# Float32 iotas, a causal select and the wide pattern's distances on GpSimd, and later size tests, in a local-attention and channel-mix kernel

## The chip, the core and the metric

The kernel runs on one core of a Trainium2 chip. The metric is the device time of one execution in microseconds. The engines are TensorE (PE, with its weight loads as PEld), VectorE (DVE), ScalarE (ACT), GpSimd (POOL) and SyncE (SP), which issues most DMAs.

## What is computed

Attention over 4 x 8 heads of 768 positions and 64 channels, with a local window, a few global positions and a distance bias, and behind it a channel mix of width 512 and 1024. `n_global` is 8 and `n_local` is 96, both given as 64-bit integers at run time.

```python
scores = q @ k.T / sqrt(D)
rel = pos[:, None] - pos[None, :]
is_global = pos[None, :] < n_global
is_local = (rel >= 0) & (rel < n_local)
dist = where(is_global & ~is_local, n_local, abs(rel))
scores = where(is_global | is_local, scores - slopes[h] * dist, -1e9)
x = softmax(scores) @ v                     # heads side by side: B, S, 512
xk, xr = (mu * x + (1 - mu) * x_prev for mu in (mu_k, mu_r))
out = sigmoid(xr @ w_r) * (relu(xk @ w_k) ** 2 @ w_v)
```

## The kernel before

A tile is 128 queries; there are 24 of them, 6 for each batch. A tile sees at most 232 keys: 8 global ones, the 96 before it, and its own 128. Per tile and pair of heads (`hp`), TensorE makes scores (L421 and L422 in the first six tiles, L424 and L425 later), VectorE adds the bias pattern and takes the row's extreme (L430), ScalarE exponentiates with the sum (L431), TensorE transposes (L461, named t_0 to t_3 by head pair), ScalarE copies the result out (L465), and TensorE multiplies by v (L486). Two tiles make a chunk of 256 columns for the channel mix: `mix` makes xk and xr (L520) and splits each into a high part (L521, ScalarE) and a low part (L522, VectorE); `channel_mix` multiplies them by the weights in three passes (L531 to L533: kp, z, vps).

The weights arrive as 64-bit words. Ten blocks (4 of w_k, 2 of w_r, 4 of w_v) are turned into floats by VectorE in three operations (L210, L211, L212 on `wa`), and split into high (L216, ScalarE) and low parts (L234 on VectorE, or L230 to L232 through TensorE). This happens in tiles 0 to 5, beside the attention of those tiles.

The bias patterns come first of all. `btmp` holds pieces of scratch: from iotas (GpSimd) come the distances; `dist0` (L149) makes `pat0`, the pattern of a batch's first tile (128 keys, L153 and L155), and `dist` (L163 to L166) makes `pat`, the wide pattern of all other tiles (232 keys, L170 on ScalarE and L172 on GpSimd, four heads each). FAR is 1e12. `read_sizes` (L78 to L80) turns the two sizes into floats. L806 to L811 test whether the sizes fit this path; the result is used at the end (L812), to choose a general path, `wide`, which does not run here. `PLAN["GO"]` names the tile and head pair behind whose L430 these tests are put; here (1, 1).

What each engine does in which order is set by a scheduler that places the instructions of all engines by a timeline of its own; `issue_after` bounds it, and SP's queue is kept in program order in the first six steps. SP's loads there are: q and k of tile 0, of tile 1, v of tile 0, two blocks of w_k, q and k of tile 2, v of tile 1, two more blocks of w_k, and so on. The q and k tiles of the first six tiles have only every second partition loaded, and the others are cleared once, by a fill on some engine (`zero_fill`, L306 to L311) that the load waits for. `ident` and `minus` (L83, L85) are identity matrices. The first ten matmuls of the kernel (L116) work on zeros and give nothing.

Of the kernel before, what the change touches and what calls it, by code (L numbers as in the profile page):

```python
# [12 lines left out]
I32 = mybir.dt.int32  # L13
U32 = mybir.dt.uint32
AF = mybir.ActivationFunctionType
ALU = mybir.AluOpType
# [9 lines left out]
GMAX = 8  # L26
BACK = 96
LMAX = BACK + 1
W = GMAX + BACK + 128
OWN = GMAX + BACK  # L30
# [13 lines left out]
    "Z": {('q', 0): 'D', ('q', 1): 'A', ('k', 1): 'A'},  # L44
    "P0": 'DADDADAD',
    "GD": 0,
    "GO": (1, 1),
    "PT": 'PAPAPAPA',
    "BEHIND": {},
    "WB": {},  # L50
# [7 lines left out]
FAR = 1.0e12  # L58
# [4 lines left out]
def tile_biased_attention_channel_mix(ctx: ExitStack, tc: tile.TileContext, qT, kT, v, n_sizes, mu_kr, w_k, w_v, w_r, q_rows, k_rows, v_rows, slopes, out):  # L63
    nc = tc.nc
    vec, act, pool, pe = nc.vector, nc.scalar, nc.gpsimd, nc.tensor
# [8 lines left out]
    ngf, nlf = sizes[:, 0:1], sizes[:, 1:2]  # L74

    def read_sizes():
        low, high = words[:, :, 0], words[:, :, 1]
        vec.tensor_copy(words, sizes_w)  # L78
        vec.scalar_tensor_tensor(sizes, low, 0.0, high, op0=ALU.is_lt, op1=ALU.add)
        vec.scalar_tensor_tensor(sizes, sizes, 4294967296.0, low, op0=ALU.mult, op1=ALU.add)  # L80
# [47 lines left out]
    def piece():  # L128
        edge.append(next(cut))
        return btmp[:, edge[-2] : edge[-1]]  # L130

    ints, flts, local, glo, dist0, dist = (piece() for _ in range(6))
    ints = ints.bitcast(I32)
    j = flts[:, 224:352]

    pool.iota(ints[:, 96:224], [[-1, 128]], base=0, channel_multiplier=1)
    pool.iota(ints[:, 224:352], [[1, 128]], base=0, channel_multiplier=0)
    pool.iota(ints[:, 0:96], [[-1, 96]], base=96, channel_multiplier=1)
    vec.tensor_copy(flts, ints)
    causal = flts[:, 96:224]  # L140
    vec.tensor_scalar(dist0, causal, 0.0, FAR, op0=ALU.is_lt, op1=ALU.mult)
    vec.tensor_max(causal, causal, dist0)
    read_sizes()


# [14 lines left out]
    with ExitStack() as later:  # L160
        if PLAN.get("GD"):
            later.enter_context(tc.issue_after(first_done.ins))
        vec.tensor_scalar(local[:, 0:96], flts[:, 0:96], nlf, FAR, op0=ALU.is_ge, op1=ALU.mult)  # L163
        vec.tensor_copy(dist[:, OWN:W], local[:, 96:224])
        vec.tensor_scalar(dist[:, 0:GMAX], glo[:, 0:GMAX], nlf, None, op0=ALU.max)
        vec.tensor_add(dist[:, GMAX:OWN], local[:, 0:96], flts[:, 0:96])  # L166
    for h in range(H):
        c = -8.0 * 2.0 ** -(h + 1)
        if PLAN.get("PT", "PAPAPAPA")[h] == "A":
# [695 lines left out]
```

## Time and profile before

| | |
|---|---|
| median of 3 runs | 495.69 us (495.29 to 499.2) |
| the profiled execution: its own time | 496.69 us |
| the profiled execution: its span | 494.9 us |
| PE busy | 485.4 us (98%), 3614 instructions |
| PEld busy | 432.0 us (87%) |
| DVE busy | 349.7 us (71%), 839 instructions |
| ACT busy | 335.7 us (68%), 852 instructions |
| POOL busy | 205.5 us (42%), 331 instructions |
| HBM read, written | 53.55 MB, 6.29 MB |

The span runs from the first to the last instruction of the core. Busy times are averages over a start, in which patterns and weights are made, and a long steady part. Matmuls are pipelined and their ends are modelled, so a busy PE is not PE at its peak.

### The profile page before, as it was taken

What the parts mean: (1) busy time and instruction counts of PE and PEld (TensorE: products, weight loads), DVE (VectorE), ACT (ScalarE), POOL (GpSimd) and SP (SyncE); (2) the same over time, 40 slices, a digit from 0 to 9 for tenths busy, and PEclk for the clock granted to TensorE, in tenths of its full rate; (3) what the DMA queues carried; (4) which work ended last, traced back from release to release, by engine and by line L of the source; (5) the groups of instructions that cost most, each with busy time, mean ns of one, the idle gap of its engine ahead of it and who ended that gap; (6) DMA issues with size and microseconds to landing.
All of it is one profiled execution on the core that took longest, in us unless ns stands there. A gap on an engine that the chain in (4) does not pass through costs nothing.

```text
span 494.9 us, 10286 instructions
## 1 busy us (share of the span) xinstructions
PE 485.4 (98%) x3614; PEld 432.0 (87%) x3614; DVE 349.7 (71%) x839; ACT 335.7 (68%) x852; POOL 205.5 (42%) x331
## 2 busy tenths in 40 slices
PE   8799999999999999999999999999999999999997
PEld 5579898898988998998998998998998998898986
DVE  7989997867677677677687686677768764464541
ACT  8889967648488568477487477576587577686370
POOL 4201051646465554644655635635546525203000
PEclk9999999999999999999999999999999999999999
DMA  6988162620616306406405405504503216656311
GB/s 237 376 284 346 35 129 82 165 88 2 172 24 160 90 7 171 115 1 162 129 1 145 129 1 136 156 1 121 152 21 103 85 23 185 213 199 227 128 43 50
DMA packets 22587, 60.59 MB, mean 122 GB/s; under 512 B 3296, under 2 KB 4576, under 8 KB 22016
## 3 DMA queue, kind: packets, MB, share of 16 engines
q1 hardware_dynamic: 22384, 59.85, 40.8%
q8 instruction: 31, 0.51, 0.4%
q14 instruction: 28, 0.23, 0.2%
q10 hardware_dynamic: 144, 0.00, 0.0%
HBM read 53.55 MB, written 6.29 MB: 121 GB/s over the span
## 4 chain that ended last, share of the span: by engine, by line
PE 92%; DVE 3%; DMA 2%; ACT 1%; issue 1%; ACTq 0%
PE vps L531 9%; PE vps L533 9%; PE vps L532 9%; PE kp L531 9%; PE kp L532 9%; PE kp L533 9%; PE av L486 8%; PE t L461 8%; PE z L531 4%; PE z L532 4%; PE z L533 4%; PE s L425 3%; PE s L424 3%; DMA qz<-in_qT_dram 2%; PE s L422 2%; PE s L421 1%
## 5 line engine op out<-in xcount | busy, mean ns | idle before, releaser
L449 POOL TENSOR_SCALAR e<-e,r 128x232 f32<-128x232 f32 (+1 forms) x144 | 68.8, 497 | 121.1 <-DVE r L443 83.1
L431 ACT ACTIVATE e<-e,nmax 128x232 f32<-128x232 f32 (+1 forms) x192 | 89.6, 469 | 37.4 <-DVE nmax L430 36.9
L531 PE MATMUL kp<-xk_hi,wk 128*128 128x256 f32 x384 | 107.9, 282 | 0.0
L532 PE MATMUL kp<-xk_lo,wk 128*128 128x256 f32 x384 | 107.3, 280 | 0.0
L533 PE MATMUL kp<-xk_hi,wk 128*128 128x256 f32 x384 | 107.2, 280 | 0.0
L430 DVE CUSTOM_DVE_ANT_0 e<-s,pat 128x232 f32<-128x232 f32 (+1 forms) x192 | 64.2, 374 | 30.4 <-PE s L425 27.1
L531 PE MATMUL vps<-wv,kk_hi 128*128 128x512 f32 (+1 forms) x200 | 76.8, 385 | 0.0
L533 PE MATMUL vps<-wv,kk_lo 128*128 128x512 f32 (+1 forms) x200 | 76.7, 383 | 0.0
L532 PE MATMUL vps<-wv,kk_hi 128*128 128x512 f32 (+1 forms) x200 | 76.4, 382 | 0.0
L532 PEld LDWEIGHTS kp<-xk_lo,wk 128*128 128x128 f32 x384 | 72.1, 188 | 0.8 <-DVE xk_lo L522 0.2
L531 PEld LDWEIGHTS kp<-xk_hi,wk 128*128 128x128 f32 x384 | 72.0, 188 | 0.7 <-ACT xk_hi L521 0.3
L533 PEld LDWEIGHTS kp<-xk_hi,wk 128*128 128x128 f32 x384 | 72.1, 188 | 0.0
L465 ACT COPY et<-t 128x256 f32<-128x256 f32 (+1 forms) x176 | 53.3, 355 | 25.1 <-PE t L461 24.9
L461 PE MATMUL t<-ident,e 128*128 128x128 f32 x352 | 54.5, 275 | 1.5 <-ACT et L465 1.4
L562 DVE TENSOR_TENSOR kk<-kp,kk 128x512 f32<-128x512 f32 x48 | 32.9, 687 | 29.7 <-ACT kk L561 29.4
L564 DVE TENSOR_TENSOR kk_lo<-kk,kk_hi 128x512 fp32r<-128x512 f32 x48 | 35.7, 747 | 24.0 <-ACT kk_hi L563 23.2
L461 PEld LDWEIGHTS t<-ident,e 128*128 128x128 f32 x352 | 40.3, 135 | 7.3 <-ACT et L465 1.6
L563 ACT CAST kk_hi<-kk 128x512 fp32r<-128x512 f32 x48 | 29.8, 623 | 21.9 <-DVE kk L562 21.6
L533 PEld LDWEIGHTS vps<-wv,kk_lo 128*128 128x128 f32 x200 | 37.6, 188 | 7.5
L531 PEld LDWEIGHTS vps<-wv,kk_hi 128*128 128x128 f32 x200 | 37.6, 189 | 6.7 <-ACT pat L576 0.2
L532 PEld LDWEIGHTS vps<-wv,kk_hi 128*128 128x128 f32 x200 | 37.7, 189 | 6.5
L424 PE MATMUL s<-kw,qh 128*128 128x232 f32 (+1 forms) x144 | 40.4, 306 | 0.0
(121 smaller groups left out, 1071.4 us busy)
## 6 DMA issues: line engine op xcount, KB each, us to landing
qraw<-in_qT_dram SPq DMA_DIRECT2D x36, 256.0 KB
kraw<-in_kT_dram SPq DMA_DIRECT2D x36, 256.0 KB
out_dram<-sig SPq DMA_DIRECT2D x23, 256.0 KB
va<-in_v_dram SPq DMA_DIRECT2D x20, 240.0 KB
vb<-in_v_dram SPq DMA_DIRECT2D x20, 208.0 KB
w<-in_w_k_dram SPq DMA_DIRECT2D x4, 1024.0 KB
w<-in_w_v_dram SPq DMA_DIRECT2D x4, 1024.0 KB
again<-in_w_k_dram SPq DMA_DIRECT2D x8, 512.0 KB
```

Source lines behind the costliest of these rows:

```text
L424: pe.matmul(o, s["qh"][:, h, :], s["kw"][:, h, c0:W], start=True, stop=False)
L430: biased[n, hp] = vec.tensor_tensor_reduce(out=e[:, :w], in0=o, in1=p[:, h, :], op0=ALU.add, op1=ALU.min, scale=-0.125, scalar=3.0e38, acc ...
L431: act.activation(e[:, :w], e[:, :w], AF.Exp, bias=s["nmax"][:, h : h + 1], scale=-1.0, accum_out=s["sum"][:, h : h + 1])
L449: pool.tensor_scalar(e[:, :w], e[:, :w], r[:, u : u + 1], 1.0, op0=ALU.mult, op1=ALU.mult)
L461: s["turned"] = pe.transpose(pt[0:p, c : c + 128], e[:, k * 128 : k * 128 + p], ident)
L465: act.copy(dst, pt[0:p, k * 256 : k * 256 + 256].rearrange("p (u q) -> p u q", u=2)[:, :, q:128])
L486: pe.matmul(o, vt[:, h * 64 : (h + 1) * 64], et[0:p, c : c + 128 - q], start=k == 0, stop=k == nb - 1)
L531: pe.matmul(o, sh, mh, start=first, stop=False)
L532: pe.matmul(o, sh, ml, start=False, stop=False)
L533: return pe.matmul(o, sl, mh, start=False, stop=last)
L562: vec.tensor_mul(kk, pv, kk)
L564: rest = vec.tensor_sub(kkl[:, 2 * fp : 2 * fp + 2, :], kk, kkh[:, 2 * fp : 2 * fp + 2, :])
```

## The change

The iotas write float32 at once, so that the cast L139 falls away. The causal part, "FAR where the key lies ahead of the query", is a select on GpSimd in place of two VectorE operations. The four operations that make `dist` go to GpSimd, two of them in a form with a second factor of 1.0. The size tests are put behind L430 of tile 8 in place of tile 1.

```diff
-    "GO": (1, 1),
+    "GO": (8, 1),
...
-    pool.iota(ints[:, 96:224], [[-1, 128]], base=0, channel_multiplier=1)
-    pool.iota(ints[:, 224:352], [[1, 128]], base=0, channel_multiplier=0)
-    pool.iota(ints[:, 0:96], [[-1, 96]], base=96, channel_multiplier=1)
-    vec.tensor_copy(flts, ints)
+    def count(o, step, base, channel):
+        pool.iota(o, [[step, o.shape[1]]], base=base, channel_multiplier=channel, allow_small_or_imprecise_dtypes=True)
+
     causal = flts[:, 96:224]
-    vec.tensor_scalar(dist0, causal, 0.0, FAR, op0=ALU.is_lt, op1=ALU.mult)
-    vec.tensor_max(causal, causal, dist0)
+    count(causal, -1, 0, 1)
+    pool.affine_select(causal, causal, [[-1, 128]], ALU.is_ge, FAR, base=0, channel_multiplier=1)
+    count(j, 1, 0, 0)
+    count(flts[:, 0:96], -1, 96, 1)
     read_sizes()
...
-        vec.tensor_scalar(local[:, 0:96], flts[:, 0:96], nlf, FAR, op0=ALU.is_ge, op1=ALU.mult)
-        vec.tensor_copy(dist[:, OWN:W], local[:, 96:224])
-        vec.tensor_scalar(dist[:, 0:GMAX], glo[:, 0:GMAX], nlf, None, op0=ALU.max)
-        vec.tensor_add(dist[:, GMAX:OWN], local[:, 0:96], flts[:, 0:96])
+        pool.tensor_scalar(local[:, 0:96], flts[:, 0:96], nlf, FAR, op0=ALU.is_ge, op1=ALU.mult)
+        pool.tensor_add(dist[:, GMAX:OWN], local[:, 0:96], flts[:, 0:96])
+        pool.tensor_scalar(dist[:, 0:GMAX], glo[:, 0:GMAX], nlf, 1.0, op0=ALU.max, op1=ALU.mult)
+        pool.tensor_scalar(dist[:, OWN:W], local[:, 96:224], 1.0, 1.0, op0=ALU.mult, op1=ALU.mult)
```

The scheduler then orders other work differently too, in about the first 115 us. Three places show it, each as a difference of one engine's order, with - for before and + for the change.

ScalarE at its very start, where it clears the q and k tiles of tile 1 (qz_182 and kz_183, each in two halves) and makes `minus`:

```order
 L309 ACT_TABLE_LOAD
 L309 CAST qz_182<-zeros 128x512 x2
-L309 CAST kz_183<-zeros 128x512 x2
+L309 CAST kz_183<-zeros 128x512
 L85 ACTIVATE minus<-ident 128x128
+L309 CAST kz_183<-zeros 128x512
 L153 ACTIVATE pat_137<-btmp 128x128 x3
 L170 ACTIVATE pat<-btmp 128x232 x4
```

The second half of the k fill now stands behind L85.

TensorE at the change from tile 1 to tile 2: t_0_370 and t_1_389 are transposes of tile 1, s_0_378 and s_1_397 are scores of tile 2, whose L421 needs the q load of tile 2 (qz_178):

```order
 L461 MATMUL t_0_370<-ident,e_1_287 128x128
 L461 MATMUL t_0_370<-ident,e_1_287 104x128
+L421 MATMUL s_0_378<-kz_183,qz_178 128x104
+L421 MATMUL s_1_397<-kz_183,qz_178 128x104
 L461 MATMUL t_1_389<-ident,e_2_316 128x128
 L461 MATMUL t_1_389<-ident,e_2_316 104x128
 L461 MATMUL t_1_389<-ident,e_3_319 128x128
 L461 MATMUL t_1_389<-ident,e_3_319 104x128
-L421 MATMUL s_0_378<-kz_183,qz_178 128x104
-L421 MATMUL s_1_397<-kz_183,qz_178 128x104
```

The two L421 have moved ahead of the four transposes t_1 of tile 1.

VectorE in tile 4, behind the L430 of its third head pair (e_5): wa_621, wa_724 and wa_848 are the weight blocks 6, 7 and 8, e_6 and e_7 the last two heads of tile 4, and xk_lo is the low part of the first chunk:

```order
+L210 TENSOR_SCALAR wa_848<-w_8_788 128x1024
+L212 SCALAR_TENSOR_TENSOR wa_621<-w_6_600,wa_621 128x1024
 L430 ISA e_6_868,nmax_599<-s_3_863,pat 128x232
 L430 ISA nmax_599 128x1
 L430 ISA e_7_871,nmax_599<-s_3_863,pat 128x232
 L430 ISA nmax_599 128x1
-L212 SCALAR_TENSOR_TENSOR wa_621<-w_6_600,wa_621 128x1024
-L522 TENSOR_TENSOR xk_lo<-mix_k,xk_hi 128x1024
-L210 TENSOR_SCALAR wa_848<-w_8_788 128x1024
 L212 SCALAR_TENSOR_TENSOR wa_724<-w_7_664,wa_724 128x1024
+L522 TENSOR_TENSOR xk_lo<-mix_k,xk_hi 128x1024
+L211 SCALAR_TENSOR_TENSOR wa_848<-w_8_788,wa_848 128x1024
```

L210 on block 8 and L212 on block 7 stood behind xk_lo and now stand ahead of it, and L212 on block 6 stands ahead of e_6 and e_7.

## Rows read from the trace of the kernel before

**Rows 1.** Busy time by stretch: stretch, its length, busy per engine (instructions), granted clock, DMA share, GB/s.

```profile
core 0: us, PE busy (x) PEld busy (x) DVE busy (x) ACT busy (x) POOL busy (x), PEclk, DMA share, GB/s
6.00:7.00 1.00, 1.00 (x8) 0.87 (x8) 1.00 (x6) 0.98 (x5) 0.71 (x2) 1.00 0.55 111
...
13.00:17.60 4.60, 1.80 (x15) 1.30 (x13) 4.20 (x15) 3.54 (x16) 1.79 (x2) 1.00 1.06 333
17.60:50.80 33.20, 33.08 (x285) 26.48 (x285) 31.74 (x76) 29.48 (x85) 4.57 (x5) 1.00 0.88 321
...
54.70:450.00 395.30, 395.30 (x2982) 357.81 (x2982) 281.01 (x655) 271.37 (x670) 189.15 (x296) 1.00 0.38 104
```

**Rows 2.** Waits of PE after 40 us: total us, times, longest.

```profile
PE s L421 <- issue: 1.0, 1, 1.0
PE row L269 <- DVE worst L267: 0.3, 1, 0.3
```

**Rows 3.** Chain that ended last, in order of time: start us, us, what.

```profile
8.84 8.69 DMA qz<-in_qT_dram
...
480.75 0.23 PE vps L532
```

**Rows 4.** Timeline 0 to 8 us: start, us, engine, line, operation [idle before <- releaser].

```profile
1.06 4.45 PE L116 MATMUL idle<-zeros 128*128 128x512 bf16 x10 [1.06 <-DVE zeros L113]
...
1.52 0.29 POOL masks.py:199 TENSOR_SCALAR_AFFINE_SELECT ident<-ident 128x128 f32<-128x128 f32 x1
1.79 1.84 POOL L306 MEMSET kz<- 128x1024 f32 x2
2.00 1.87 DVE L139 CAST btmp<-btmp 128x352 f32<-128x352 int32 x1
3.52 1.13 ACT L309 CAST kz<-zeros 128x512 f32<-128x512 bf16 x2
4.56 0.31 ACT L85 ACTIVATE minus<-ident 128x128 fp32r<-128x128 f32 x1
4.68 0.47 SPq L339 DMA_DIRECT2D kz<-in_kT_dram  x1
...
6.21 1.71 POOL L172 TENSOR_SCALAR pat<-btmp 128x232 bf16<-128x232 f32 x4 [2.30 <-DVE btmp L164]
6.63 1.24 ACT L170 ACTIVATE pat<-btmp 128x232 bf16<-128x232 f32 x4
7.09 0.28 DVE L430 CUSTOM_DVE_ANT_0 e<-s,pat 128x128 f32<-128x128 f32 x1
7.99 0.25 POOL L297 TENSOR_SCALAR k_first<-kz 128x64 f32<-128x64 f32 x1
```

**Rows 5.** Timeline 14 to 28 us, PE, POOL and DVE.

```profile
14.94 1.21 POOL L297 TENSOR_SCALAR kz<-k_first 128x64 f32<-128x64 f32 x1
15.54 0.66 PE L461 MATMUL t<-ident,e 128*128 128x128 f32 x4 [1.39 <-ACT et L465]
17.66 0.66 PE L421 MATMUL s<-kz,qz 128*128 128x104 f32 x4 [1.47 <-DMA qz<-in_qT_dram]
20.32 0.14 DVE L811 TENSOR_SCALAR okf<-okf 128x1 f32<-128x1 f32 x1
20.39 0.38 DVE L430 CUSTOM_DVE_ANT_0 e<-s,pat 128x232 f32<-128x232 f32 x1
27.43 0.40 DVE L430 CUSTOM_DVE_ANT_0 e<-s,pat 128x232 f32<-128x232 f32 x1 [1.11 <-PE s L422]
```

**Rows 6.** Timeline 53 to 57 us, DVE and PE.

```profile
53.44 1.21 DVE L522 TENSOR_TENSOR xk_lo<-mix_k,xk_hi 128x1024 fp32r<-128x1024 f32 x1
54.57 0.68 DVE L210 TENSOR_SCALAR wa<-w 128x1024 int32<-128x1024 int32 x1
54.70 0.38 PE L532 MATMUL kp<-xk_lo,wk 128*128 128x256 f32 x1
55.17 1.21 DVE L212 SCALAR_TENSOR_TENSOR wa<-w,wa 128x1024 int32<-128x1024 int32 x1
56.31 0.39 DVE L430 CUSTOM_DVE_ANT_0 e<-s,pat 128x232 f32<-128x232 f32 x1
```

More of the change, by code (lines that the diff above doesn't have):

```diff
@@ L130, in piece @@
         return btmp[:, edge[-2] : edge[-1]]
-    ints, flts, local, glo, dist0, dist = (piece() for _ in range(6))
-    ints = ints.bitcast(I32)
+    _, flts, local, glo, dist0, dist = (piece() for _ in range(6))
     j = flts[:, 224:352]
-    pool.iota(ints[:, 96:224], [[-1, 128]], base=0, channel_multiplier=1)
-    pool.iota(ints[:, 224:352], [[1, 128]], base=0, channel_multiplier=0)
-    pool.iota(ints[:, 0:96], [[-1, 96]], base=96, channel_multiplier=1)
-    vec.tensor_copy(flts, ints)
+    def count(o, step, base, channel):
+        pool.iota(o, [[step, o.shape[1]]], base=base, channel_multiplier=channel, allow_small_or_imprecise_dtypes=True)
     causal = flts[:, 96:224]
-    vec.tensor_scalar(dist0, causal, 0.0, FAR, op0=ALU.is_lt, op1=ALU.mult)
-    vec.tensor_max(causal, causal, dist0)
+    count(causal, -1, 0, 1)
+    pool.affine_select(causal, causal, [[-1, 128]], ALU.is_ge, FAR, base=0, channel_multiplier=1)
+    count(j, 1, 0, 0)
+    count(flts[:, 0:96], -1, 96, 1)
     read_sizes()
```

## The prediction, made before the change was run

> **What bounds the kernel now.** I read the stretches first, then what TensorE waited for, then the chain, then the start row by row. In the table by stretch, TensorE is busy 395.30 of the 395.30 us from 54.70 on, 33.08 of 33.20 between 17.60 and 50.80, but only 1.80 of 4.60 before 17.60 [rows 1]. After 40 us it waits twice, 1.0 us and 0.3 us [rows 2]. So nearly everything behind 54.7 us is matmuls end to end: what is lost or won before that time is carried to the end, and nothing behind it can give much back. The change works in the first 60 us, where three things set the pace.
>
> First, the vector work on the patterns: the cast L139 takes 1.87 us and the first biased scores (L430) begin at 7.09, behind the pattern work [rows 4]. Second, the loads: the chain spends 8.69 us on the q load of tile 2, issued at 8.84 [rows 3]; it lands behind the first two blocks of w_k, and TensorE stands 1.47 us before L421 starts at 17.66, having stood 1.39 us just before [rows 5]. Third, VectorE's weight work: from 27.43 on it has no row with an idle time ahead of it worth naming; at 53.44 it makes xk_lo, done at 54.65, and TensorE's first matmul on xk_lo starts at 54.70 [rows 6]. From there TensorE never waits again. So the question is: when does VectorE finish xk_lo, and when does the q load of tile 2 land?
>
> **The change part by part.**
>
> *The start.* L139 goes (1.87 us [rows 4]), with L141, L142 and the four operations of the wide pattern, so VectorE reaches L430 earlier. It cannot before the first scores exist, which wait for a k load at about 5.9; from 7.09 that is 0.8 us or a little more. What is late next is the q load of tile 2. Its issue waits for TensorE's scores of tile 0, so it moves up by the same 0.8 us, but the queue's order ahead of it is unchanged and the engines are full: DMA share 1.06 up to 17.60 [rows 1]. I therefore let it land where it does, and the 0.8 us become a longer wait of TensorE: worth nothing (bounds: 0 and -0.8).
>
> *GpSimd's share.* The iotas keep their count. The causal select is not in the trace; ident's select on the same 128x128 shape takes 0.29 [rows 4]. The four operations of the wide pattern run on GpSimd instead: 0.39 to 0.43 each by L172 (1.71 for four of 128x232) [rows 4], about 1.6 us and done near 6 us; ScalarE takes up its half of that pattern (L170) at 6.63 now [rows 4], so no loss. The upper bound is the 128x64 copy at 14.94 that took 1.21 us beside VectorE's work, against 0.25 for the one at 7.99 [rows 4, 5]: four of those are 4.8 us. I take the low end, since L172 has the same form and ran while VectorE made its own patterns; the other is a rival.
>
> The Trainium skill (SBUF — State Buffer, Who interferes with whom) says VectorE and GpSimd share a port pair as an exclusive lock, so whoever comes second waits for the other's whole instruction. The trace agrees: L139 overlaps GpSimd's two fills and ends 0.24 us after them. By the rule the four moved operations and VectorE's short ones take turns, which would eat the 0.8 us at the start and leave the sum as it is.
>
> *The k fill.* ScalarE clears the k tile in two halves (1.13 us for both), and L85 follows; SP issues that tile's k load at 4.68, when the fill is done [rows 4]. The new order puts L85 (0.31) between the halves. The loads have a gap just there (DMA share 0.55 from 6 to 7 us [rows 1]) and everything behind queues up, w_k and the q load of tile 2 included: +0.25 us (bounds 0 and 0.31).
>
> *The size tests.* L806 to L811 leave VectorE's early work. Two of them stand before a wait and are free; four cost what they push back the next row, as L811 at 20.32 does to L430 at 20.39 [rows 5]: 0.07 each, -0.25 us in all (at most 4 x 0.14). In tile 8 they cost the same on a VectorE that is not waited for.
>
> *What the scheduler does with it.* TensorE's transposes t_1 of tile 1 now stand behind the L421 that waits for the q load, so 0.44 us of work that ran before the wait runs after it; the scores of tile 2's second half come earlier, so VectorE's 1.11 us wait at 27.43 [rows 5] shrinks. But TensorE is busy 33.08 of 33.20 [rows 1] and has work added, so of the 1.11 I credit only -0.2 (bounds 0 and -1.1). The term that matters: two weight operations that followed xk_lo now precede it. L210 on block 8 takes 54.57 to 55.17, L212 on block 7 55.17 to 56.31 [rows 6]: +1.74 us on VectorE ahead of xk_lo, while TensorE has only tile-5 scores and transposes to do, and the second of these also wait for L430s that stand behind L210 and L212. The bound below is nothing, if TensorE still had 1.74 us of work at that point; but now it starts 0.05 us after xk_lo is done, so I take it all.
>
> The sum: 0 + 0.25 - 0.25 - 0.2 + 1.74 = +1.5 us on xk_lo, kept to the end. The profiled execution took 496.69 us (span 494.9), 1.0 above the median of 495.69; that run would take 498.2, and the median goes to **497.2 us**. By its own bounds the sum runs from +0.2 to +2.0: 495.9 to 497.7.
>
> **The rivals.**
>
> *The early start survives.* If the q load lands 0.8 us earlier with its issue, and the 1.74 us find cover, the kernel gains: 495.69 - 0.8 = 494.9 us, or about no change where only one of them holds. For it: TensorE did wait 1.47 us on just that load. Against: the saturated queue, and the 0.05 us at 54.7.
>
> *TensorE's clock falls.* Now TensorE stands from 14.15 to 15.54, runs t_1 for 0.66 us, and stands again until L421 at 17.66 [rows 5]. Moved behind L421, t_1 leaves TensorE with nothing from about 13.8 to 17.9: 4 us instead of two waits of 1.4 and 1.5. At the kernel's start ten matmuls of 512 columns took 4.45 us [rows 4], the pace of 1.2 GHz; one of 512 columns at 480.75 takes 0.23, that of 2.4 GHz [rows 3]. If the clock fell in the longer gap and took as long as then to rise, TensorE would lose half of 4.45: 497.2 + 2.2 = 499.4 us. It decides only if the gap really closes up to 4 us; both present waits left the granted clock at 1.00 [rows 1]. The Trainium skill (TensorE: Matmul & The Clock Gate, HAM oscillation — how this bites in real kernels) has the clock fall back when matmuls wait for a DMA too long; no row here shows a fall.
>
> *The wide pattern comes late.* With four operations of 1.21 us, it is done at 4.2 + 4.8 = 9.0, and ScalarE's L170 (1.24), which stands ahead of all its exponentials, ends at 10.3 instead of 7.87. ScalarE has 1.06 us idle before 17.60 [rows 1], so some 1.3 us remain: 498.5 us. It decides above 0.6 us per operation.
>
> *More than 5 us lost* would take several such stops; I see no place for it.
>
> **How the numbers follow.** The forecast 0.57; the early start, whole or in part, 0.23; the clock 0.12; the late pattern 0.04; the rest 0.04. The range to hold 8 in 10: from 494.7, a little under the first rival, to 499.5, over the second. One per cent of this kernel, 5 us, is about what a measurement tells from no change. Only the upper end of the clock rival and a part of the rest reach it: faster 0.02, same 0.92, slower 0.06.
>
> **What would show it.** Right: L430's first start near 6.3; L421 of tile 2 still at 17.5 to 18.0 with a wait of some 4 us ahead of it; xk_lo finished near 56, TensorE idle just before, and full from there on. Wrong: L421 of tile 2 before 17.2 (the loads were not what held it); xk_lo's first matmul at or before 54.7; a granted clock under 1.00 after 17 us; L170 ending after 8 us; or a TensorE wait of over 0.5 us behind 60 us, where I counted none.

## The result, and the profile after

The changed kernel takes 500.21 us (median of 22 runs, 496.07 to 502.06); the kernel before, timed beside it, 496.24 us (22 runs, 494.64 to 499.9). The ratio is 1.0056, 95% interval 1.0036 to 1.0077. It is smaller than the ratio of the two medians (1.0080), as the times of each kernel fall into two groups, on which more below, and the changed kernel has most of its runs in the slower one; the ratio of the means is 1.0061. That is slower by some 2.8 us, clear of the noise but within the one per cent that counts as no change. On the 495.69 us from which the forecast was made, the ratio gives 498.5 us: 1.3 above the forecast of 497.2 and inside the range of 494.7 to 499.5. The median of 500.21 itself lies above that range, since the kernel before is 0.55 us slower here and the medians lie further apart than the ratio says. The profiled execution took 500.58 us with a span of 498.7 us (before: 496.69 and 494.9), so 3.8 us have to be found.

By stretch (columns as in [rows 1]):

```profile
core 0: us, PE busy (x) PEld busy (x) DVE busy (x) ACT busy (x) POOL busy (x), PEclk, DMA share, GB/s
13.00:17.60 4.60, 1.16 (x11) 0.90 (x9) 3.49 (x13) 2.56 (x12) 0.86 (x2) 1.00 1.05 309
17.60:19.00 1.40, 0.62 (x3) 0.66 (x4) 1.40 (x2) 0.71 (x3) 0.00 (x0) 0.70 1.00 395
19.00:20.00 1.00, 1.00 (x7) 0.99 (x7) 1.00 (x2) 0.00 (x0) 0.00 (x0) 0.50 1.06 352
21.00:22.00 1.00, 1.00 (x8) 1.00 (x8) 0.30 (x1) 0.96 (x2) 0.00 (x0) 0.71 1.00 410
...
50.80:54.70 3.90, 3.30 (x31) 2.51 (x31) 3.90 (x9) 2.93 (x9) 1.45 (x1) 1.00 0.01 5
54.70:58.00 3.30, 2.65 (x17) 1.91 (x18) 3.30 (x8) 3.30 (x12) 0.00 (x0) 1.00 0.01 2
58.00:100.00 42.00, 42.00 (x309) 37.35 (x311) 35.19 (x75) 28.59 (x67) 14.28 (x13) 1.00 0.47 113
```

Two stretches differ. Between 13 and 17.6 us TensorE is busy 1.16 us instead of 1.80, and then its granted clock, the next to last column but one, goes from 1.00 to 0.50, from 2.4 to 1.2 GHz, until past 21 us. And from 50.8 to 58 us TensorE has holes, where before it was full from 54.7 on. From 58 us it is full again, as nearly everything is matmuls there.

What TensorE waited for between 10 and 60 us (columns as in [rows 2]), and its rows around the q load of tile 2, which answer to [rows 5]:

```profile
PE s L421 <- DMA qz<-in_qT_dram: 4.2, 1, 4.2
PE t L461 <- ACT e L431: 0.6, 1, 0.6
```

```profile
13.34 0.82 PE L461 MATMUL t<-ident,e 128*128 128x128 f32 x6
18.38 1.15 PE L421 MATMUL s<-kz,qz 128*128 128x104 f32 x4 [4.22 <-DMA qz<-in_qT_dram]
```

The two short waits have become one of 4.22 us, as the order of TensorE let expect, and four L421 then take 1.15 us where they took 0.66. The chain, which answers to [rows 3], has the q load longer by 0.86 us:

```profile
8.69 9.55 DMA qz<-in_qT_dram
```

The start, on VectorE, GpSimd, ScalarE and SyncE's queue, answering to [rows 4]:

```profile
3.41 0.55 DVE L78 CAST words<-sizes_w 128x4 f32<-128x4 int32 x1 [1.32 <-DMA sizes_w<-in_n_sizes_dram]
6.95 0.28 DVE L430 CUSTOM_DVE_ANT_0 e<-s,pat 128x128 f32<-128x128 f32 x1
4.52 0.72 POOL L163 TENSOR_SCALAR btmp<-btmp,sizes 128x96 f32<-128x96 f32 x1 [0.42 <-DVE sizes L80]
6.39 1.24 ACT L170 ACTIVATE pat<-btmp 128x232 bf16<-128x232 f32 x4
4.87 0.47 SPq L339 DMA_DIRECT2D kz<-in_kT_dram  x1
```

In the kernel before, the first of these was

```profile
3.79 0.15 DVE L78 CAST words<-sizes_w 128x4 f32<-128x4 int32 x1
```

L430 starts 0.14 us earlier than before (7.09), not 0.8. VectorE no longer casts the patterns, but then it waits 1.32 us for the sizes' load, and L78 takes 0.55 us instead of 0.15. GpSimd's four distance operations (the first took 0.72) were done in time, and L170 ends at 7.63.

The stage before the first chunk's xk_lo, VectorE, ScalarE and TensorE, answering to [rows 6]:

```profile
52.56 0.38 DVE L430 CUSTOM_DVE_ANT_0 e<-s,pat 128x232 f32<-128x232 f32 x1
53.20 0.68 DVE L210 TENSOR_SCALAR wa<-w 128x1024 int32<-128x1024 int32 x1
53.56 1.06 ACT L521 CAST xk_hi<-mix_k 128x1024 fp32r<-128x1024 f32 x1
55.58 1.21 DVE L212 SCALAR_TENSOR_TENSOR wa<-w,wa 128x1024 int32<-128x1024 int32 x1
56.72 1.21 DVE L522 TENSOR_TENSOR xk_lo<-mix_k,xk_hi 128x1024 fp32r<-128x1024 f32 x1
57.37 0.48 ACT L431 ACTIVATE e<-e,nmax 128x232 f32<-128x232 f32 x1
57.53 0.90 PE L461 MATMUL t<-ident,e 128*128 128x128 f32 x4 [0.59 <-ACT e L431]
58.19 0.36 PE L532 MATMUL kp<-xk_lo,wk 128*128 128x256 f32 x1
```

The kernel before has the first of these (e_4 of tile 4) and xk_hi at:

```profile
48.62 1.06 ACT L521 CAST xk_hi<-mix_k 128x1024 fp32r<-128x1024 f32 x1
...
51.02 0.39 DVE L430 CUSTOM_DVE_ANT_0 e<-s,pat 128x232 f32<-128x232 f32 x1
```

So of the 3.49 us by which TensorE's first matmul on xk_lo is late (54.70 to 58.19), 1.54 stand already at e_4 and 1.95 are lost between e_4 and that matmul: 3.68 us there before, 5.63 now. Those are the two parts that the experiments take apart. In this trace the matmul does not wait for xk_lo, which is done at 57.93, 0.26 us before it: the chain runs through ScalarE, from xk_hi over its last exponentials to the transposes at 57.53.

### The profile page after: what moved, and what is told of

The parts are those of the page before. It is cut to its first block, busy times and chain, and to the rows that moved or that the text cites. A ratio compares the mean times of both kernels' runs of the same rounds, so it can differ in the third digit from the quotient of the medians.

```text
span 498.7 us, 10285 instructions
## 1 busy us (share of the span) xinstructions
PE 486.9 (98%) x3614; PEld 433.6 (87%) x3614; DVE 348.0 (70%) x832; ACT 335.6 (67%) x852; POOL 204.0 (41%) x336
## 4 chain that ended last, share of the span: by engine, by line
PE 91%; DVE 4%; DMA 2%; ACT 1%; issue 1%; ACTq 0%; DVEq 0%
PE kp L531 9%; PE kp L533 9%; PE kp L532 9%; PE vps L531 9%; PE vps L533 9%; PE vps L532 9%; PE av L486 7%; PE t L461 7%; PE z L531 4%; PE z L533 4%; PE z L532 4%; PE s L425 3%; PE s L424 3%; DMA qz<-in_qT_dram 2%; PE s L422 1%; DVE e L430 1%
## 5 line engine op out<-in xcount | busy, mean ns | idle before, releaser
L449 POOL TENSOR_SCALAR e<-e,r 128x232 f32<-128x232 f32 (+1 forms) x144 | 65.6, 473 | 126.3 <-DVE r L443 84.0
L430 DVE CUSTOM_DVE_ANT_0 e<-s,pat 128x232 f32<-128x232 f32 (+1 forms) x192 | 64.4, 373 | 31.1 <-PE s L425 26.3
L461 PE MATMUL t<-ident,e 128*128 128x128 f32 x352 | 56.1, 277 | 0.8 <-ACT e L431 0.6
L564 DVE TENSOR_TENSOR kk_lo<-kk,kk_hi 128x512 fp32r<-128x512 f32 x48 | 36.7, 765 | 23.7 <-ACT kk_hi L563 22.9
L400 DVE TENSOR_TENSOR ql<-qraw,qh 128x1024 fp32r<-128x1024 f32 x18 | 33.2, 1846 | 10.2 <-POOL qh L297 9.3
```

Of the source, the lines that this page charges most:

```text
L400: vec.tensor_sub(ql, s["qr"], qh)
L430: biased[n, hp] = vec.tensor_tensor_reduce(out=e[:, :w], in0=o, in1=p[:, h, :], op0=ALU.add, op1=ALU.min, scale=-0.125, scalar=3.0e38, acc ...
L449: pool.tensor_scalar(e[:, :w], e[:, :w], r[:, u : u + 1], 1.0, op0=ALU.mult, op1=ALU.mult)
L461: s["turned"] = pe.transpose(pt[0:p, c : c + 128], e[:, k * 128 : k * 128 + p], ident)
L564: rest = vec.tensor_sub(kkl[:, 2 * fp : 2 * fp + 2, :], kk, kkh[:, 2 * fp : 2 * fp + 2, :])
```

## The experiments

Any edit makes the scheduler order everything behind it anew. So in all experiments a list of issue-order edges holds every instruction of every engine where it stands in the kernel named, and only what is named moves. Rows of diffs are instructions in issue order. The granted clock on record for a run is a mean over the execution; "lost" below are the runs with 0.997 or less, the others have 0.998 to 1.000. The experiments ran in three groups of four, at different times and on three chips, each with the kernel before beside it, so medians of different groups are compared with care, and the ratios beside them. Of the 22 runs of the kernel before beside the changed one no clock is on record.

| kernel | runs | lost the clock | median, all | median, clock kept | ratio to before (95%) |
|---|---|---|---|---|---|
| before, beside the first four | 25 | 8 | 496.74 | 496.55 | |
| before, beside the next four | 35 | 15 | 496.68 | 496.20 | |
| before, beside the last four | 35 | 16 | 497.43 | 496.20 | |
| after | 22 | 16 | 500.21 | 497.51 | 1.0056 (1.0036 to 1.0077) |
| fill_gap | 12 | 0 | 499.14 | 499.14 | 1.0041 (1.0026 to 1.0057) |
| t1_first | 6 | 6 | 500.68 | | 1.0074 (1.0050 to 1.0097) |
| xklo_first | 8 | 7 | 499.99 | 498.41 | 1.0061 (1.0038 to 1.0084) |
| gap_in_before | 12 | 11 | 499.13 | 495.33 | 1.0032 (1.0008 to 1.0056) |
| ops_only | 12 | 9 | 497.93 | 496.24 | 1.0007 (0.9985 to 1.0029) |
| late_order | 12 | 10 | 498.43 | 496.56 | 1.0028 (1.0001 to 1.0054) |
| head_order | 12 | 8 | 499.39 | 497.98 | 1.0042 (1.0018 to 1.0066) |
| q_first | 12 | 8 | 497.28 | 495.77 | 0.9994 (0.9969 to 1.0019) |
| fill_late | 12 | 0 | 497.44 | 497.44 | 1.0001 (0.9975 to 1.0026) |
| fill_ops | 12 | 0 | 496.99 | 496.99 | 0.9991 (0.9968 to 1.0015) |
| fill_before | 12 | 0 | 496.74 | 496.74 | 0.9991 (0.9968 to 1.0014) |
| fill_q | 12 | 2 | 496.15 | 496.02 | 0.9972 (0.9948 to 0.9996) |

**fill_gap**, the clock taken out of the 4 us gap:

```diff
 L461 t_0 of tile 1, x4
+idle<-zeros 128x512, x16      (idle = ps_a.tile([128, 512], F32, name="idle", tag="av"))
 L421 s_0, s_1 of tile 2
```

> The changed kernel with every engine's order held as it was, and 16 matmuls of zeros (512 columns) put behind the last transpose t_0 of tile 1, in TensorE's 4.2 us wait for the q load of tile 2; at 0.21 to 0.23 us each they end near 17.7, before the load lands at 18.2, and delay nothing. Theory A (the lost time beyond the forecast is TensorE's clock, which falls because TensorE stands 4 us): granted clock 1.00 from 17 us on, L421 of tile 2 takes 0.6 us instead of 1.15, and the time goes from 500.2 to about 497.4, what the runs of the changed kernel took that kept the clock. Rival (the late q load and the 1.74 us of weight work ahead of xk_lo make the whole loss): no change, 500 us, with a clock that falls or not.

```profile
14.02 3.62 PE L465 MATMUL idle<-zeros 128*128 128x512 bf16 x16
18.57 0.66 PE L421 MATMUL s<-kz,qz 128*128 128x104 f32 x4 [0.94 <-DMA qz<-in_qT_dram]
```

No run of 12 lost the clock, against 16 of 22, and L421 takes 0.66 us again. But the time is 499.14, not 497.4: filling the gap gives back 1.07 us of the median, or 0.75 by the ratios, whose intervals overlap. The expectation compared with those runs of the changed kernel that kept their clock; but in the profiled executions of these kernels L421, which needs the q load, starts anywhere from 16.4 to 18.8 us (q_first and fill_q, which load in another order, left out), and where the load lands early the gap is short too. So a kept clock there may also mark an early load. Here the load landed at 18.5 in the profiled execution, and the 16 matmuls ended 0.94 us before it; whether they cost something in another way is open.

**t1_first**, TensorE's order at tile 2 undone:

```diff
 L461 t_0 of tile 1, x4
+L461 t_1 of tile 1, x4
 L421 s_0, s_1 of tile 2
-L461 t_1 of tile 1, x4
```

> The changed kernel with the four transposes t_1 of tile 1 ahead of the two L421 of tile 2 again, as in the kernel before; nothing else moves. TensorE then has two gaps of about 1.4 and 2.2 us instead of one of 4.2. Theory A: the clock stays at 1.00, 497.4 us or 0.4 less, as 0.44 us of work runs ahead of the wait. Rival (it is the time of the q load that counts, not the gap): 500 us, or 499.8.

```profile
14.40 0.69 DVE L210 TENSOR_SCALAR wa<-w 128x1024 int32<-128x1024 int32 x1 [2.12 <-DMA w<-in_w_k_dram]
16.95 0.66 PE L461 MATMUL t<-ident,e 128*128 128x128 f32 x4 [2.77 <-ACT et L465]
18.80 0.66 PE L421 MATMUL s<-kz,qz 128*128 128x104 f32 x4 [1.20 <-DMA qz<-in_qT_dram]
```

The rival's number came, 500.68, but not for its reason alone: all 6 runs lost the clock. The transposes wait 2.77 us for a copy et of ScalarE (1.39 in the kernel before, [rows 5]), which starts 1.41 us later than in the kernel before (16.54 against 15.13). In the new order it stands behind one exponential more, about 0.5 us; the other 0.94 us are that the first of them starts at 15.58 instead of 14.64, behind VectorE, whose L210 in this execution got its block of w_k at 14.40 instead of 13.40. So the gap is not made by TensorE's order alone; ScalarE's new order, and a load that comes later, leave it little to do there.

**gap_in_before**, the converse in the kernel before:

```diff
 L461 t_0 of tile 1, x4
-L461 t_1 of tile 1, x4
 L421 s_0, s_1 of tile 2
+L461 t_1 of tile 1, x4
```

> The kernel before with the two L421 of tile 2 ahead of the four transposes t_1 of tile 1 on TensorE, as in the changed kernel; nothing else moves. TensorE then stands from 14.15 to about 17.6, 3.5 us, in one piece. Theory A: the granted clock falls to half in some runs or in all, and those take 2 to 4 us more than 495.7, so 498 to 500; where it stays, 495.7 to 496.2. Rival (the order of TensorE alone costs nothing): 495.7 in every run.

```profile
6.04 3.87 PE L422 MATMUL s<-kz,qz 128*128 128x128 f32 x16 [0.53 <-DVE btmp L149]
...
18.48 1.15 PE L421 MATMUL s<-kz,qz 128*128 128x104 f32 x4 [3.21 <-DMA qz<-in_qT_dram]
```

11 of 12 lost the clock (8 of 25 in the kernel before beside it) and the median rises to 499.13. So the longer gap alone raises how often the clock is lost, and 2.4 us of the median follow (1.6 by the ratio). In this execution the first matmuls of tile 0 also ran at about half pace until 9.9 us, on which more below.

**xklo_first**, VectorE's order before xk_lo undone:

```diff
-L210 wa, block 8
 L212 wa, block 6
 L430 e_6, e_7 of tile 4
-L212 wa, block 7
 L522 xk_lo
+L210 wa, block 8
+L212 wa, block 7
```

> The changed kernel with xk_lo (L522) of the first chunk ahead of L210 on block 8 and L212 on block 7, as in the kernel before; nothing else moves. Theory B (the 1.74 us of VectorE work are paid in full): xk_lo starts 1.7 us earlier and the time is 1.7 us less, 498.5 us; TensorE's clock still falls in most runs. Rival (TensorE was late by then for other reasons, so xk_lo is not what it waits for): less than 0.5 us gained.

```profile
50.28 0.38 DVE L430 CUSTOM_DVE_ANT_0 e<-s,pat 128x232 f32<-128x232 f32 x1
52.69 1.21 DVE L522 TENSOR_TENSOR xk_lo<-mix_k,xk_hi 128x1024 fp32r<-128x1024 f32 x1
51.28 1.06 ACT L521 CAST xk_hi<-mix_k 128x1024 fp32r<-128x1024 f32 x1
55.26 0.91 PE L461 MATMUL t<-ident,e 128*128 128x128 f32 x4 [0.59 <-ACT e L431]
55.92 0.36 PE L532 MATMUL kp<-xk_lo,wk 128*128 128x256 f32 x1
```

The rival is right: 499.99, a gain of 0.2 us, and none by the ratios (1.0061 and 1.0056). xk_lo now starts 2.41 us after e_4 instead of 4.16, and yet TensorE's first matmul on it starts 5.64 us after e_4, as before the edit (5.63). The transposes t_3 of tile 4 stand ahead of it on TensorE, and they wait for ScalarE's last exponentials, which the late xk_hi pushes back. Two chains, VectorE's and ScalarE's, end within 0.3 us of each other; taking one away leaves the other.

**late_order** and **head_order** divide the new order at tile 3: late_order has the head of the changed kernel and behind it, on all engines, the order of the kernel before; head_order the reverse. For late_order, on ScalarE and VectorE in tile 4:

```diff
+L521 xk_hi
 L498 x
 L465 et, x4
-L521 xk_hi
 L431 e_4, e_5
```

```diff
+L520 mix_k, x3
 L210 wa, block 7
+L520 mix_k
-L234 wr
 L211 wa, block 6
-L520 mix_k, x3
+L234 wr
 L211 wa, block 7
-L520 mix_k
 L430 e_4, e_5
-L210 wa, block 8
-L212 wa, block 6
 L430 e_6, e_7
+L212 wa, block 6
-L212 wa, block 7
 L522 xk_lo
+L210 wa, block 8
+L212 wa, block 7
```

> The changed kernel with its own order up to tile 3, and the order of the kernel before from there on, on all engines; so xk_hi, xk_lo and the weight operations of the first chunk stand as in the kernel before, while the 4 us gap of TensorE stays. Theory C: the stage ahead of xk_lo's first matmul gives back the 1.95 us that it lost (from e_4 of tile 4 to that matmul 3.7 us instead of 5.6): 498.2 us, with the clock still down in most runs. Rival (TensorE makes up for a late first chunk): 500 us.

> The changed kernel with the order of the kernel before up to tile 3, and its own order from there on; so TensorE's long gap is two short ones again, while xk_hi and xk_lo of the first chunk come late. Theory C: the clock is kept in two runs of three, and those take 496.5 + 1.95 = 498.4 us. Rival (the head's order makes the whole loss): 496.5 us.

Of late_order, VectorE, ScalarE and TensorE:

```profile
51.30 0.39 DVE L430 CUSTOM_DVE_ANT_0 e<-s,pat 128x232 f32<-128x232 f32 x1
53.71 1.21 DVE L522 TENSOR_TENSOR xk_lo<-mix_k,xk_hi 128x1024 fp32r<-128x1024 f32 x1
48.90 1.05 ACT L521 CAST xk_hi<-mix_k 128x1024 fp32r<-128x1024 f32 x1
54.98 0.38 PE L532 MATMUL kp<-xk_lo,wk 128*128 128x256 f32 x1
```

Of head_order, VectorE and TensorE:

```profile
51.32 0.39 DVE L430 CUSTOM_DVE_ANT_0 e<-s,pat 128x232 f32<-128x232 f32 x1
55.48 1.21 DVE L522 TENSOR_TENSOR xk_lo<-mix_k,xk_hi 128x1024 fp32r<-128x1024 f32 x1
56.74 0.39 PE L532 MATMUL kp<-xk_lo,wk 128*128 128x256 f32 x1
```

late_order comes out as expected: 498.43, 1.78 us less than the changed kernel (1.4 by the ratios), with the clock lost in 10 of 12; from e_4 to the first matmul on xk_lo it is 3.68 us again. Its profiled execution kept a granted clock of 1.00 through a wait of 3.54 us before L421 of tile 2 (the profile names a VectorE operation that ended just then; what L421 needs is the q load):

```profile
17.72 0.66 PE L421 MATMUL s<-kz,qz 128*128 128x104 f32 x4 [3.54 <-DVE wa L210]
```

head_order keeps the late stage (5.42 us) and takes 499.39. Its runs with a kept clock have 497.98, near the 498.4 expected, but 8 of 12 lost it, its profiled execution among them, though the waits there before L421 are 0.87 and 1.19 us. So the length of the one gap does not decide alone whether the clock falls.

**ops_only**, the operations without the order: every engine as in the kernel before, except for the operations that the diff itself moves or replaces. Against the changed kernel, behind tile 3 as late_order, and ahead of it among others on ScalarE and TensorE:

```diff
 ACT: L309 kz, first half
-     L85 minus
      L309 kz, second half
+     L85 minus
 PE:  L461 t_0 of tile 1
+     L461 t_1 of tile 1
      L421 s_0, s_1 of tile 2
-     L461 t_1 of tile 1
```

> The changed kernel's operations in the kernel before's order: the iotas, the select and the four distance operations stay on GpSimd and the size tests behind tile 8, but TensorE, ScalarE, SyncE, VectorE and GpSimd issue everything else as in the kernel before. Theory C (the loss comes from the new order of the engines alone, the operations cost nothing): about 496.5 us, what the kernel before takes, with the clock kept in about two runs of three as there. Rival (the four operations on GpSimd or the later k fill cost the time): 498 us or more. A gain of the shorter start would show as 496 or less.

497.93 us, ratio 1.0007 (0.9985 to 1.0029); with a kept clock 496.24 (three runs), against 496.20 before. The median is nearer to the rival's 498 than to the 496.5 expected, with the clock lost in 9 runs of 12; by the ratio the operations cost or bring nothing beyond the interval of 1.1 us. The kernel before beside it lost the clock in 15 of 35; with so few runs it stays open whether the new operations have a part in that.

**q_first**, on top of ops_only; block 1 of w_k loaded later (and begun accordingly):

```diff
-    "LOADS": (2, 2, 2, 2, 3, 3, ...
+    "LOADS": (1, 1, 1, 1, 3, 3, ...
```

```diff
 SP:  DMA w_0
-     DMA w_1
      DMA qz, kz of tile 2; va, vb of tile 1
+     DMA w_1
 DVE:-L210, L211 wa, block 1
      L430 e_0 to e_3 of tile 2
     +L210, L211 wa, block 1
```

> As ops_only, and the load of the second block of w_k is issued behind the q and k loads of tile 2 (and the v load of tile 1) instead of ahead of them; VectorE's first two operations on that block move behind the first four L430 of tile 2. If the q load is late because of that block ahead of it in the queues, it lands near 14.5 us instead of 17.5, TensorE has no wait above 1.5 us, the clock is kept in every run, and the time is 495 us (494.5 to 495.8), since VectorE's 31.7 busy of 33.2 us then sets the pace. Rival (the block is as urgent as the q load): 496.5 us or more, with VectorE waiting for the block at 18 us.

```profile
15.23 0.65 PE L461 MATMUL t<-ident,e 128*128 128x128 f32 x4 [1.17 <-ACT et L465]
15.97 1.00 PE L421 MATMUL s<-kz,qz 128*128 128x104 f32 x4
```

In this execution the load is there earlier with the block out of its way: L421 starts at 15.97 and waits for no DMA (at 15.16 in fill_q, which loads in the same order). The time is 497.28, not the 495 expected, about that of the kernel before, since the clock still falls in 8 of 12 runs, with one wait of 1.17 us left.

**The last four** put matmuls of zeros into the gaps, so that orders and operations can be compared without the clock: fill_late is late_order with the 16 of fill_gap; fill_ops and fill_before have 3 behind t_0 and 6 behind t_1 of tile 1, in ops_only and in the kernel before; fill_q has 4 behind t_0, in q_first.

```diff
+        if n == 1 and hp < 2:
+            if hp == 0:
+                state["idle"] = ps_a.tile([128, 512], F32, name="idle", tag="av")
+            for i in range((3, 6)[hp]):
+                pe.matmul(state["idle"], zeros[:, 0:128], zeros.unsqueeze(1).broadcast_to([128, 2, 256]), start=True, stop=True)
```

> late_order with the 16 matmuls of zeros of fill_gap behind t_0 of tile 1. If the clock and the late order are two separate losses, both are gone: the clock is kept in every run and the time is 499.1 (fill_gap) less 1.8 (what late_order gave back), 497.3 us. If they are one loss seen twice: no better than late_order, 498.4 us.

> ops_only (the change's operations in the kernel before's order) with matmuls of zeros in TensorE's two gaps: 3 behind t_0 and 6 behind t_1 of tile 1. The clock is kept in every run, so that the operations can be compared without it: 496.2 us, the runs of ops_only that kept the clock. If the shorter start is worth anything, it is less than fill_before by up to 0.8 us; if the operations on GpSimd cost something, more.

> The kernel before with the same matmuls of zeros in the same two gaps, 3 behind t_0 and 6 behind t_1 of tile 1, its order held. About 4 runs in 10 of the kernel before lose the clock and 2.3 us; here none should: median 496.0 to 496.5, and no run above 497.5. If the matmuls themselves delay the scores: 497 us.

> q_first with 4 matmuls of zeros behind t_0 of tile 1, in its one gap of 1.17 us. The runs of q_first that kept the clock took 494.8 to 497.2 us, those that lost it 497.0 to 498.6. If that gap is what loses the clock there, every run keeps it now and the median is 495.5 to 495.8, below the kernel before. If a gap of that length is not the cause, the clock still falls in most runs: 497.3 us.

In the first three no run lost the clock. So without it, by the medians and by the ratios to the kernel before beside them, in us:

| part | difference | by medians | by ratios |
|---|---|---|---|
| the late order | fill_gap less fill_late | 1.70 | 2.0 |
| the order of the head | fill_late less fill_ops | 0.45 | 0.5 |
| the operations | fill_ops less fill_before | 0.25 | 0.0 |
| the clock in the changed kernel | after less fill_gap | 1.07 | 0.75 |
| the clock in the kernel before | before less fill_before | 0.69 | 0.45 |

Only the late order stands clear of the intervals (those of fill_gap and fill_late just touch). The first four less the fifth make 2.8 us in either column, but that is no check: each term is the difference of two neighbours, and the sum is the changed kernel less the kernel before whatever lies between. What the table shows is the shares: the late order makes most of the loss, and the clock, which falls in both kernels, 0.3 to 0.4 us of the difference between them.

fill_late met its 497.3; fill_ops and fill_before came out 0.8 and 0.2 us above what was expected, and one run of fill_before took 498.21 where none above 497.5 was expected, so the matmuls of zeros may cost some tenths themselves. fill_q, at 496.15, lies between its two expectations (2 of 12 still lost the clock) and is the fastest version of all: 0.9972 of the kernel before (0.9948 to 0.9996), about 1.4 us. TensorE is full from 13 to 17.6 us there, and what it gained meets VectorE further on (columns as in [rows 1]):

```profile
48.00:49.00 1.00, 0.66 (x6) 0.41 (x4) 1.00 (x2) 0.76 (x4) 0.00 (x0) 1.00 0.04 8
49.00:50.00 1.00, 0.00 (x0) 0.00 (x0) 1.00 (x4) 0.31 (x2) 0.00 (x0) 1.00 0.00 0
50.00:51.00 1.00, 0.68 (x3) 0.71 (x4) 1.00 (x7) 1.00 (x5) 0.00 (x0) 0.71 0.00 0
```

From 48.7 us TensorE has nothing to do for 1.7 us while VectorE is full, and in this execution the clock falls there instead of at 18 us.

## Why the prediction was right, and where it was not

**What held.** The forecast was a kernel slower by 1.5 us, most of it 1.74 us in the stage ahead of xk_lo; the change costs 2.8 us by the ratio, and 1.7 to 2.0 of them are the new order of that stage and what lies behind it. The question at the end of the first part, when xk_lo is done and when the q load of tile 2 lands, was the right one. TensorE stood 4.22 us ahead of L421, as the order showed (some 4 us were forecast); it was full behind 58 us, and L170 ended at 7.63, so the late pattern fell away. Against it stood, of the signs it named, L421 of tile 2 (18.38, not 17.5 to 18.0), xk_lo (done at 57.9, not near 56), L430's first start (6.95, not near 6.3) and a granted clock under 1.00 after 17 us. The 1.3 us between forecast and result are several terms, each smaller than the intervals: the head's order, the clock's share, and two gains that no run shows. The bounds were not worked through: those written at the terms give -0.8 + 0 - 0.56 - 1.1 + 0, so -2.5 at the low end of the sum and not the +0.2 stated; the range to hold was not built on that end.

**The start** was to be 0.8 us earlier and was 0.14. The limit that I named, the first scores, was not it: VectorE waits for the sizes' load until 3.41, and in the kernel before it came to L78 only 0.38 us later, at 3.79. Since the start was counted at nothing, the sum did not suffer. L78 ends 0.07 us behind GpSimd's fill of kz (2.94 to 3.89) that runs beside it, much as L139 ended 0.24 us behind two fills; the rule of the Trainium skill (SBUF — State Buffer, Who interferes with whom) that VectorE and GpSimd take turns at a shared port is consistent with its 0.55 us.

**The k fill** moved the k load by 0.19 us (4.68 to 4.87), under the 0.25 of the sum. The q load of tile 2 landed 0.7 us later in the profiled execution, but it varies by more than 2 us between executions, so no run here shows what the 0.19 did to it.

**The size tests and VectorE's wait** (-0.25 and -0.2): VectorE's wait at 27.43 was still 1.08 us (at 27.55), and another of 1.25 came at 21.70, because the scores came late. ops_only shows no gain from the tests beyond its interval.

**The 1.74 us.** The size was right and the account of it too narrow. The late order costs 1.7 to 2.0 us by runs and traces, and in head_order, where the clock was back by then, xk_lo is what TensorE waits for, 0.05 us after its end, and the stage takes 5.42 us against 3.68: 1.74 more. In the changed kernel itself xk_lo was not the last to come. But I read only VectorE's rows. ScalarE's xk_hi moved as well, from 2.40 us ahead of e_4 to 1.00 behind it, and its exponentials end as late as xk_lo does, so undoing VectorE's two operations gave 0.2 us. The step that I left out was to ask what else reaches that matmul in the new order; that the two chains end together, so that the size came out all the same, is luck. No run moved xk_hi and xk_lo back alone: late_order exchanges all that stands behind tile 3.

**The clock** is what I judged most wrongly. I made its fall a rival with a chance of 0.12, on the words that it "decides only if the gap really closes up to 4 us; both present waits left the granted clock at 1.00", although the gap was a part of my own forecast. One execution with a granted clock of 1.00 was read as the rule: over 95 runs the kernel before loses the clock in 39, though its profiled execution kept it through waits of 1.4 and 1.5 us, and the changed kernel loses it in 16 of 22. Of the three runs at hand before, one took 499.2 us, 3.5 above the median; its clock is not on record, but over the 95 runs no run with a kept clock took more than 497.6. The price was 2.2 us; in one and the same kernel, runs that lost it took 1.4 to 3.3 us more than runs that kept it (medians, kernels with two or more of each), a part of which may be a late load. The Trainium skill (TensorE: Matmul & The Clock Gate, HAM oscillation — how this bites in real kernels) has the clock fall back when matmuls wait for a DMA too long; after and gap_in_before agree, at 4.2 and 3.2 us. But the profiled execution of late_order kept it through 3.54 us, and that of q_first, one of the 8 of 12 that lost it, did so with a single wait of 1.17 us there, and for a copy, not a DMA: no length of a wait in the profiled executions told whether the clock is kept. Filling the gaps told, with none lost in the 48 runs of fill_gap, fill_late, fill_ops and fill_before.

That the forecast came out near all the same has a reason that I did not give: the kernel before pays for the clock too. With my price of 2.2 us, 16 of 22 runs against 39 of 95 make a difference of 0.7 us, and 1.5 + 0.7 = 2.2 against the 2.8 measured; by the filled kernels it is 0.3 to 0.4. In the two profiled executions, one with the clock lost and one with it kept, 1.5 + 2.2 = 3.7 stands against 3.8, partly by luck, as the smaller terms erred. What stays open is why some runs of one and the same program keep the clock, and why the six runs of the changed kernel that kept it (497.51) are faster than fill_gap (499.14).

## What to carry to other kernels

Where a gap is left in the matmuls of a start-up stage, count the clock's fall as part of the forecast, and ask many runs, not one profile, how often it happens, in the kernel before as well; filling the gaps with matmuls of zeros (9 to 16 here) shows what the rest costs without it. Where a scheduler orders the program, a small change moves everything behind it: hold the order and exchange it piece by piece to tell the operations from the order (here the order cost 2.1 to 2.5 us and the operations at most 0.25, which is within the noise). And before undoing one late operation, look for the second chain that ends beside it.

## What was not expected of the hardware

The first matmuls after the start may run at about half pace for longer than the ten of zeros: in gap_in_before the 16 matmuls of tile 0 took 3.87 us in one piece, 0.23 us from one to the next instead of 0.12, where before they took 1.13 and 1.16 with a wait between, and SyncE then issued the q load of tile 2 at 9.95 instead of 8.84, as it waits for those scores. ops_only shows the same. The granted clock reads 1.00 throughout that stretch, so there only the pace of the rows tells it; whether it is the clock that slows them is not shown.

The same queue order gave the same load very different landings, though issued at 8.84 and 8.83: L421 of tile 2, which needs it, waits for it until 17.66 in the kernel before and starts at 16.36 in fill_before, with no wait in front at all:

```profile
15.06 1.46 PE L466 MATMUL idle<-zeros 128*128 128x512 bf16 x6
16.36 0.59 PE L421 MATMUL s<-kz,qz 128*128 128x104 f32 x4
```
